# An FFN behind a recurrent cross-attention: the third and fourth weight transfers cut in quarters, batch 0's softmax by quarters, a rewritten opening order

## The chip, the cores and the metric

The kernel runs on one core of a Trainium2 chip. The metric is device time in microseconds (us) of one execution, median over several runs. A profile of one execution goes with it: its "span" is the part in which the core's engines have instructions, and the execution's own time is a little longer. The engines are TensorE (PE in the profile, PEld for its weight loads), VectorE (DVE), ScalarE (ACT), GpSimd (POOL) and SyncE (SP), which only issues transfers. Each runs its own list of instructions in order and waits for others by semaphores.

## What is computed

There are 8 batches of 8 heads, with 512 rows of x and 32 rows of state per head, 64 wide. Two attentions read across: the state rows as queries' partners for x, and the x rows for the state. Their outputs, 544 rows a batch with 8 × 64 = 512 columns, go through a gated FFN of width 1536.

```
scores = scale * x @ state^T            a  = softmax(scores)          xread = a  @ state
scores2 = scale * state @ x^T           a2 = softmax(scores2)         sread = a2 @ x
y = concat([xread, sread], rows)        # 8 * 544 rows of 512 columns
gate = 1 / (1 + exp(-(y @ w_gate)));    val = y @ w_val
out = (gate * val) @ w_out
```

The inputs and the output are float32; the kernel multiplies in bfloat16 and adds up in float32.

## The kernel before

**Work per batch.** Since xread is a @ state, the kernel never forms it: it multiplies state by the gate and value weights first (the tile SW, 256 rows by 2 × 1536), and then SW by a. In steps, by the helpers' names:

- xT: x of a batch, transposed. For batches 0 and 1 by TensorE (`xT_mm`, L132) and a copy out of PSUM (`xT_cp`, L135), for later ones by DMA transposes on SP's queue (`at_xT_dma`, L140), after a cast to bfloat16 (`cast_xp` L91 for batch 0, `cast_x` L116).
- S: scores by TensorE (`S_mm`, L147 and L156), half a batch's heads or rows at a time; `S_exp` (L167, ScalarE) makes the exponentials E1; `n_sum` (L181, L183) sums them and takes the reciprocal on VectorE; `n_mul` (L200) multiplies into ab. `n_sums` and `n_muls` (L187 to L193) do both halves at once.
- aT: ab transposed, by TensorE (`aT_mm` L207, `aT_cp` L217) for batches 0 and 1, by DMA transposes (`aT_dma`, L221) later.
- rd: sread, by `at_Eb` (L173, four casts of E1 on GpSimd), `rd_mm` (L235 to L241) and `rd_fin` (L246, L248).
- SW: `sw_visit(b, lo, n)` multiplies state by n columns of the weights from column lo. Called with w = 0 (gate) or 1 (value) it takes up to 512 columns of one (`sw_mm`, L259); without, 256 columns of both (`sw_pair`, L266). A visit is eight matmuls into two PSUM banks; `sw_cp` (L303) evicts each of the two on ScalarE (act) or VectorE (vec). For batches from 2 on, `sw_wide` makes three visits.
- gv: `gv_mm(b, f, ...)` is the product of SW and aT for 128 of the 1536 columns: two matmuls for the gate, two for the value. `gv_th` (L327) takes tanh on ScalarE, `gv_glu` (L332) joins gate and value on VectorE.
- out: `out_mm` (L348), four matmuls of a third of a 128-row block; after the third, the result is scaled (L352) and stored (L356).

**Transfers.** x of batch 0 and of batches from 4 on come on SP's queue, the first state rows on ScalarE's; everything else on GpSimd's queue: x of batch 1 (`load_xh`, L96), weights with a cast to bfloat16 (`load_w(w, lo, n)`, L100), w_out in three blocks (`load_wo`, L107), state (`load_sb`, L394), x of batches 2 and 3 (`load_x`, L78). These issues stand in GpSimd's list among its casts and multiplications. A transfer of the queue may also wait for the eighth one ahead of it, whose semaphore it takes over.

**Order.** All engines' work is written out by hand: the order of the calls is the order of each engine's list. Ahead of the loop over batches 2 to 8 (from L681) stands one long list of calls (L430 to L680), for all of batches 0 and 1, the outputs of batch 0 and the preparation of batch 2. `warm(n, place)` (L384) puts in n matmuls on zeros. PSUM's eight banks are places: GV (2 banks), OU (1), SWP (4) and AT (1); a matmul into a bank waits for the last reader of what was there. `gate(tile)` (L104) copies one element on GpSimd, so that what stands behind it in GpSimd's list waits for that tile.

The list before opens so: x of batch 0 in quarters of its heads (6, 0, 4, 2), the casts on ScalarE, VectorE and GpSimd, scores in halves of which each is made in two parts, and exponentials, sums and multiplications by halves:

```
    S_mm(0, 1, GV, (0,))
    S_mm(0, 0, SWP, (0,))
    S_mm(0, 1, SWP, (1,))
    S_exp(0, 1)
    n_sum(0, 1)
    S_mm(0, 0, AT, (1,))
```

The weights come as columns 256 to 511 of value and of gate, then 512 columns from 1024 of gate and of value, from 512 of value, from 512 of gate, and the first 256 of each.

Of the kernel before, what the change touches and what calls it, by code (L numbers as in the profile page):

```python
# [16 lines left out]
def kernel(  # L17
# [92 lines left out]
    def zero(t, eng):  # L110
        (nc.gpsimd if eng is pool else nc.vector).memset(t, 0.0)
# [22 lines left out]
    def xT_cp(b, j, cp, n=1):  # L134
        cp(xT_tile(b)[:, j:j + n], held["xT", b, j])  # L135
# [28 lines left out]
    def S_exp(b, i):  # L164
        if b not in E1s:
            E1s[b] = ap_.tile((128, 4, 2, 128), FP, name="E1")
        nc.scalar.activation(half(b, i, E1s), held["S", b, i].rearrange("p c e j n -> p (c e j) n" if b > 1 else "p c e j n -> p (c e) j n"),  # L167
                             AF.Exp, scale=scale)
# [133 lines left out]
    def sw_cp(b, lo, w, e, cp):  # L302
        cp(*sw_left.pop((b, lo, w, e)))  # L303
# [76 lines left out]
    def warm(n, place):  # L380

        ps = place[0].tile((128, 512), FP, name="warm", tag=place[1])
        for _ in range(n):
            nc.tensor.matmul(ps.rearrange("p (r k) -> p r k", r=4), wm, wm.unsqueeze(1).to_broadcast((128, 4, 128)), start=True, stop=True)  # L384
# [12 lines left out]
    def cast_s(q, cp):  # L397
        sbs[q] = stg.tile((128, 1, 4, D), BF, name="sb", bufs=1)
        cp(sbs[q], sfs[q])
# [27 lines left out]

    ident_e = ident.rearrange("p (g e u) -> p e g u", e=2, u=8)
    pre = wp.tile((128, 2), FP, name="pre")
    load_xp(0, nc.sync, 6, 2)  # L430
    nc.vector.memset(wm, 0.0)  # L431
    warm(1, GV)
    warm(2, GV)
    warm(4, SWP)
    zero(sTz, pool)
    load_xp(0, nc.sync, 0, 2)
    load_s(0, nc.scalar)
    zero(sTd, vec)
# [12 lines left out]
    load_w(1, 256, 256)
    cast_xp(0, pool, 4, 2)
    xT_mm(0, 0, GV)
    xT_cp(0, 0, act)
    xT_mm(0, 2, SWP)
    warm(1, SWP)
    xT_cp(0, 3, vec)
    load_w(0, 256, 256)
    xT_cp(0, 2, vec)
    S_mm(0, 1, GV, (0,))  # L460
    load_xp(0, nc.sync, 2, 2)
    S_mm(0, 0, SWP, (0,))
    cast_xp(0, act, 2, 2)
    xT_mm(0, 1, OU)
    zero(sbz, vec)
    xT_cp(0, 1, vec)
    S_mm(0, 1, SWP, (1,))
    warm(1, GV)
    S_exp(0, 1)
    n_sum(0, 1)  # L470
    S_mm(0, 0, AT, (1,))
    warm(1, OU)
    load_w(0, 1024, 512)
    xT_mm(1, 0, SWP, 2)
    warm(2, AT)
    S_exp(0, 0)
    warm(1, SWP)
    warm(1, SWP)
    xT_mm(1, 2, OU, 2)
    xT_cp(1, 0, act, 2)  # L480
    S_mm(1, 0, SWP)
    xT_cp(1, 2, act, 2)
    S_exp(1, 0)
    n_sum(0, 0)
    n_mul(0, 0, vec)
    load_w(1, 1024, 512)
    nc.vector.memset(ones, 1.0)
    at_Eb(0)
    rd_mm(0, GV)
    n_mul(0, 1, vec)  # L490
    S_mm(1, 1, GV)
    S_exp(1, 1)
    aT_mm(0, AT)
    sw_visit(0, 256, 256)
    load_sb(2)
    sw_cp(0, 256, 2, 0, act)
    rd_fin(0)
    aT_cp(0, 0, vec)
    aT_cp(0, 1, vec)
    sw_visit(1, 256, 256)  # L500
    load_w(1, 512, 512)
    sw_cp(0, 256, 2, 1, vec)
    sw_cp(1, 256, 2, 0, act)
    warm(2, OU)
    at_Eb(1)
    n_sums(1)
    gv_mm(0, 2, GV)
    gv_th(0, 2)
    sw_cp(1, 256, 2, 1, act)
    rd_mm(1, OU)  # L510
# [24 lines left out]
    gv_mm(0, 8, SWP)
    gv_glu(0, 11)
    gv_mm(0, 10, GV)
    gv_th(0, 8)
    gv_th(0, 10)
    sw_cp(1, 1024, 1, 1, vec)  # L540
    load_w(1, 0, 256)
    gv_glu(0, 8)
    sT_mm(2, AT)
    sw_visit(1, 512, 512, 1)
    sw_cp(1, 512, 1, 1, act)
    gv_mm(1, 9, SWP)
    gv_th(1, 9)
    sT_cp(2, act)
    gv_mm(1, 11, SWP)
    gv_glu(0, 10)  # L550
    gv_th(1, 11)
    load_x(2, nc.gpsimd)
    rd_fin(1)
    gv_glu(1, 9)
    gv_mm(1, 2, GV)
    sw_cp(1, 512, 1, 0, act)
    sw_visit(1, 512, 512, 0)
    gv_glu(1, 11)
    gv_th(1, 2)
    sw_visit(0, 512, 512, 0)  # L560
    sw_cp(1, 512, 0, 1, act)
    gv_glu(1, 2)
    sT_mm(1, AT)
    sw_cp(1, 512, 0, 0, act)
    sw_cp(0, 512, 0, 1, vec)
    gv_mm(1, 10, GV)
    sw_visit(0, 512, 512, 1)
    gv_th(1, 10)
    sw_cp(0, 512, 0, 0, vec)
    gv_mm(1, 6, SWP)  # L570
    load_wo(1)
    sw_cp(0, 512, 1, 1, act)
    gv_th(1, 6)
    gv_glu(1, 10)
    gv_mm(1, 8, GV)
    sw_cp(0, 512, 1, 0, vec)
    load_wo(0)
    gv_glu(1, 6)
    gv_th(1, 8)
    gv_glu(1, 8)  # L580
    sT_mm(3, OU)
    sw_visit(1, 0, 256)
    sw_cp(1, 0, 2, 0, act)
    sw_visit(0, 0, 256)
    load_wo(2)
    gv_mm(0, 4, GV)
    sw_cp(1, 0, 2, 1, vec)
    sw_cp(0, 0, 2, 0, vec)
    cast_x(2, vec, 0, 4)
    gv_mm(1, 4, SWP)  # L590
    gv_th(0, 4)
    sw_cp(0, 0, 2, 1, act)
    gv_mm(0, 0, SWP)
    gv_glu(0, 4)
    sT_cp(3, act)
    gv_th(0, 0)
    gv_glu(0, 0)
    gv_mm(0, 5, GV)
    gv_mm(1, 7, SWP)
    gv_th(0, 5)  # L600
    gv_glu(0, 5)
    gv_th(1, 7)
    gv_glu(1, 7)
    gv_th(1, 4)
    gv_mm(0, 7, GV)
    gv_th(0, 7)
    gv_glu(0, 7)
    gv_mm(0, 1, SWP)
    gv_th(0, 1)
    gv_mm(1, 1, SWP)  # L610
    gv_glu(0, 1)
    gv_mm(1, 3, GV)
    gv_th(1, 1)
    gv_mm(1, 5, SWP)
    gv_glu(1, 4)
    gv_th(1, 3)
    gv_glu(1, 3)
    sT_cp(1, act)
    gv_mm(0, 6, GV)
    gv_th(0, 6)  # L620
    out_mm(0, 0, AT)
    cast_x(2, pool, 4, 4)
    gv_th(1, 5)
    at_xT_dma(2)
    gv_glu(0, 6)
    out_mm(0, 2)
    out_mm(0, 1, GV)
    gv_mm(0, 9, SWP)
    gv_th(0, 9)
    out_mm(0, 3)  # L630
    gv_glu(1, 5)
    pad(2, 6)
    S_mm(2, 0, GV)
    gv_glu(1, 1)
    gv_glu(0, 9)
    S_exp(2, 0)
    S_mm(2, 1, OU)
    S_exp(2, 1)
    n_sum(2, 0)
    n_sum(2, 1)  # L640
    out_mm(0, 4)
    out_mm(0, 5)
    n_mul(2, 0, vec)
    out_mm(0, 6, GV)
    load_x(3, nc.gpsimd)
    at_Eb(2)
    n_mul(2, 1, pool)
    sw_wide(2, 1)
    sw_cp(2, 1, 1, 0, act)
    aT_dma(2, 0)  # L650
    sw_cp(2, 1, 0, 0, vec)
    rd_mm(2, GV)
    sw_cp(2, 1, 1, 1, act)
    rd_fin(2)
    out_mm(0, 8)
    sw_cp(2, 1, 2, 1, vec)
    gv_mm(1, 0, SWP)
    nc.scalar.activation(pre[:, 0:1], ones, AF.Exp)
    aT_dma(2, 1)
    gv_th(1, 0)  # L660
    sw_cp(2, 1, 2, 0, vec)
    gv_glu(1, 0)
    sw_cp(2, 1, 0, 1, act)
    cast_x(3, pool, 4, 4)
    cast_x(3, act, 0, 4)
    out_mm(0, 7, GV)
    sw_wide(2, 0)
    at_xT_dma(3)
    sw_cp(2, 0, 2, 0, vec)
    out_mm(0, 10)  # L670
    out_mm(0, 9)
    sw_cp(2, 0, 1, 0, act)
    sw_cp(2, 0, 2, 1, act)
    sw_cp(2, 0, 0, 1, vec)
    out_mm(0, 11)
    load_x(4, nc.sync)
    sw_cp(2, 0, 0, 0, vec)
    gate(xTs[2][:, 0, 3, 0:1])
    nc.gpsimd.memset(xs[:, :, :, D:], 1.0)
    sw_cp(2, 0, 1, 1, vec)  # L680

    for b in range(2, B + 1):
        nb = b + 1 if b + 1 < B else None
# [87 lines left out]
```

## Time and profile before

| what | us |
|---|---|
| median of 3 runs | 222.56 (222.18 to 223.69) |
| the profiled execution | 222.21 |
| its span | 220.4 |
| TensorE busy | 214.4 |
| ScalarE busy | 129.0 |
| VectorE busy | 118.1 |
| GpSimd busy | 53.5 |

TensorE's granted clock is at its full value in all 40 slices of the span. In the profile a line such as "L259 PE MATMUL swp<-wgv,sTd 64*32 64x512 bf16" names the line of the kernel, the engine, the operation, the tile written and the tiles read, and the shape. Several records of one kind that follow each other are merged ("x8"). In the chain of waits each piece is the one that released the next, traced back from the last instruction; the tile names in it are those that the piece writes. Matmuls overlap in the pipeline, so one of 512 columns has 0.38 us from start to end while four of them take 0.86 us of the chain.

### The profile page before, as it was taken

What the parts mean: (1) busy time and instruction counts of PE and PEld (TensorE: products, weight loads), DVE (VectorE), ACT (ScalarE), POOL (GpSimd) and SP (SyncE); (2) the same over time, 40 slices, a digit from 0 to 9 for tenths busy, and PEclk for the clock granted to TensorE, in tenths of its full rate; (3) what the DMA queues carried; (4) which work ended last, traced back from release to release, by engine and by line L of the source; (5) the groups of instructions that cost most, each with busy time, mean ns of one, the idle gap of its engine ahead of it and who ended that gap; (6) DMA issues with size and microseconds to landing.
All of it is one profiled execution on the core that took longest, in us unless ns stands there. A gap on an engine that the chain in (4) does not pass through costs nothing.

```text
span 220.4 us, 4641 instructions
## 1 busy us (share of the span) xinstructions
PE 214.4 (97%) x1779; PEld 104.3 (47%) x1801; DVE 118.1 (54%) x209; ACT 129.0 (59%) x241; POOL 53.5 (24%) x90
## 2 busy tenths in 40 slices
PE   8899999999999999999999999999999999999994
PEld 3554444443444444444544454445444444566744
DVE  1899897486366446544574458344844344322301
ACT  4688977367675667565765667476656444432311
POOL 8787010370324054003600090005100000000001
PEclk9999999999999999999999999999999999999999
DMA  6999999853699445947452215230131111111113
GB/s 197 201 204 196 275 221 158 172 176 60 156 272 245 62 117 164 205 120 211 133 157 45 95 23 152 54 113 3 50 93 57 49 54 65 65 57 48 49 34 112
DMA packets 41910, 27.11 MB, mean 123 GB/s; under 512 B 24000, under 2 KB 38080, under 8 KB 41888
## 3 DMA queue, kind: packets, MB, share of 16 engines
q1 hardware_dynamic: 32544, 18.95, 34.4%
q0 software_dynamic: 9056, 7.67, 19.9%
q10 hardware_dynamic: 288, 0.20, 0.6%
q8 instruction: 14, 0.23, 0.5%
q14 instruction: 8, 0.07, 0.2%
HBM read 18.35 MB, written 8.91 MB: 124 GB/s over the span
## 4 chain that ended last, share of the span: by engine, by line
PE 93%; DVE 4%; issue 1%; ACT 1%
PE outp L348 38%; PE gvp L317 38%; PE gvp L320 5%; PE swp L259 4%; PE warm L384 2%; PE swp L266 1%; PE Sp L147 1%; PE outp L370 1%; PE rdp L235 1%; DVE rs L181 1%; DVE ab L193 1%; DVE rs L187 1%; PE aTp L207 1%; PE Sp L156 0%; DVE ab L200 0%
## 5 line engine op out<-in xcount | busy, mean ns | idle before, releaser
L332 DVE SCALAR_TENSOR_TENSOR glu<-th,gvp 128x512 bf16<-128x512 f32 (+1 forms) x108 | 70.4, 656 | 84.4 <-ACT th L327 69.4
L348 PE MATMUL outp<-wo,glu 128*128 128x512 bf16 x374 | 95.7, 379 | 1.2
L317 PE MATMUL gvp<-aT,SW 128*128 128x512 bf16 x384 | 96.7, 380 | 0.0
L327 ACT ACTIVATE th<-gvp 128x512 f32<-128x512 f32 (+1 forms) x108 | 61.7, 575 | 59.7 <-PE gvp L317 47.4
L317 PEld LDWEIGHTS <-SW 128*128 128x128 bf16 x384 | 36.1, 98 | 47.9 <-issue 5.6
L348 PEld LDWEIGHTS <-glu 128*128 128x128 bf16 x396 | 37.9, 98 | 42.1 <-issue 0.4
L303 ACT CAST SW<-swp 128x512 bf16<-128x512 f32 x70 | 39.2, 584 | 6.1 <-PE swp L259 4.7
L352 ACT ACTIVATE res<-outp 128x512 f32<-128x512 f32 x33 | 19.7, 597 | 15.2 <-PE outp L348 15.0
L303 DVE CAST SW<-swp 128x512 bf16<-128x512 f32 x26 | 17.3, 683 | 1.0 <-PE swp L266 0.8
L104 POOL COPY pre<-th 128x1 f32<-128x1 f32 x5 | 0.9, 187 | 69.4 <-ACT th L327 69.4
L361 POOL DMA_DIRECT2D out_dram<-res x2 | 1.1, 549 | 60.4 <-ACT res L352 60.4
L173 POOL CAST Eb<-E 128x256 bf16<-128x256 f32 x32 | 11.7, 400 | 12.9 <-ACT E L167 12.9
L116 POOL CAST xb<-xf 128x1024 bf16<-128x1024 f32 x10 | 10.4, 1059 | 11.1 <-DMA xf<-in_x_dram 7.6
L320 PE MATMUL gvp<-XS,wgv 128*128 128x256 bf16 x96 | 11.9, 273 | 0.0
L320 PEld LDWEIGHTS <-wgv 128*128 128x128 bf16 x96 | 9.4, 98 | 3.0
L167 ACT ACTIVATE E<-Sp 128x512 f32<-128x512 f32 x16 | 9.6, 604 | 1.9 <-PE Sp L147 1.0
L224 POOL CAST xs<-xf 128x1024 bf16<-128x1024 f32 x10 | 10.2, 1045 | 0.0
L181 DVE TENSOR_REDUCE rs<-E 128x16 f32<-128x512 f32 x14 | 9.4, 672 | 1.2 <-ACT E L167 1.2
L200 DVE TENSOR_TENSOR ab<-E,ri 128x512 bf16<-128x512 f32 x13 | 8.9, 696 | 0.0
L259 PE MATMUL swp<-wgv,sTc 64*32 64x512 bf16 x192 | 7.6, 381 | 0.0
L384 PE MATMUL warm<-wm 128*128 128x512 bf16 x17 | 6.4, 497 | 1.0 <-DVE wm L431 1.0
L147 PEld LDWEIGHTS <-xT 128*128 128x128 bf16 x96 | 4.3, 98 | 2.6
(71 smaller groups left out, 93.3 us busy)
## 6 DMA issues: line engine op xcount, KB each, us to landing
out_dram<-res SPq DMA_DIRECT2D x24, 256.0 KB, 3.2
xf<-in_x_dram SPq DMA_DIRECT2D x4, 1024.0 KB, 7.2
xf<-in_x_dram POOLq DMA_DIRECT2D x2, 1024.0 KB, 9.1
out_dram<-res SPq DMA_DIRECT2D x15, 128.0 KB, 1.9
wo<-in_moe_w_out_dram POOLq DMA_DIRECT2D x3, 512.0 KB, 13.9
xf<-in_x_dram SPq DMA_DIRECT2D x4, 256.0 KB, 3.9
wgv<-in_moe_w_gate_dram POOLq DMA_DIRECT2D x2, 512.0 KB, 8.0
wgv<-in_moe_w_val_dram POOLq DMA_DIRECT2D x2, 512.0 KB, 9.5
```

What stands on the lines that cost most here:

```text
L116: cp(xbs[b].rearrange("p c h d -> p h c d")[:, lo:lo + n], (xhs if b in xhs else xfs)[b][:, lo:lo + n])
L173: nc.gpsimd.tensor_copy(Ebs[b][:, c], E1s[b][:, c])
L181: nc.vector.tensor_reduce(grp(b, rs), half(b, i, E1s), AX.X, ALU.add)
L259: nc.tensor.matmul(pss[e][j * Ns:(j + 1) * Ns, o:o + n], sTc[rows, b, j] if b > 1 else sTd[rows, b, 2 * j + e, e], (wg, wv)[w][rows, j, lo ...
L303: cp(*sw_left.pop((b, lo, w, e)))
L317: nc.tensor.matmul(ps, SWs[b][:, g, w, fs], aTs[b][:, :, g], start=(g == 0), stop=(g == 1))
L320: nc.tensor.matmul(ps, (wg, wv)[w][:, j, fs], XS[:, :, j], start=(j == 0), stop=(j == 3))
L327: nc.scalar.activation(th, held["gv", b, f][0], AF.Tanh, scale=0.5)
L332: nc.vector.scalar_tensor_tensor(glus[b][:, f], held["th", b, f], 1.0, held["gv", b, f][1], ALU.add, ALU.mult)
L348: nc.tensor.matmul(ops[b, c], glus[b][:, f, c * 128:(c + 1) * 128], wo[:, f], start=(f == 0), stop=(f == NF - 1))
L352: nc.scalar.activation(res, ops[b, c], AF.Copy, scale=0.5)
L384: nc.tensor.matmul(ps.rearrange("p (r k) -> p r k", r=4), wm, wm.unsqueeze(1).to_broadcast((128, 4, 128)), start=True, stop=True)
```

## The change

Four helpers are new: scores, exponential, sum with reciprocal, and multiplication for a quarter of batch 0's heads (two heads of eight, all rows).

```diff
+    def Sq_mm(b, j, place):
+        ps = held["Sq", b, j] = place[0].tile((128, 4, 2, Ns), FP, name="Sp", tag=place[1])
+        for c in range(4):
+            e, c2 = c // 2, c % 2 * 2
+            nc.tensor.matmul(ps[:, c2:c2 + 2, e], xTs[b][:, j, c], sTd[:, b, 2 * j + e], start=True, stop=True)
+
+    def quarter(b, j, t):
+        return t[b].rearrange("p c e (j n) -> p (c e) j n", n=Ns)[:, :, j]
+
+    def Sq_exp(b, j):
+        if b not in E1s:
+            E1s[b] = ap_.tile((128, 4, 2, 128), FP, name="E1")
+        nc.scalar.activation(quarter(b, j, E1s), held["Sq", b, j].rearrange("p c e n -> p (c e) n"), AF.Exp, scale=scale)
+
+    def nq_sum(b, j):
+        rs = ap_.tile((128, 8), FP, name="rsq", bufs=4)
+        nc.vector.tensor_reduce(rs, quarter(b, j, E1s), AX.X, ALU.add)
+        ri = held["riq", b, j] = ap_.tile((128, 8), FP, name="riq", bufs=4)
+        nc.vector.reciprocal(ri, rs)
+
+    def nq_mul(b, j, eng):
+        if b not in abs_:
+            abs_[b] = ap_.tile((128, 4, 2, 128), BF, name="ab")
+        (nc.gpsimd if eng is pool else nc.vector).tensor_tensor(quarter(b, j, abs_), quarter(b, j, E1s),
+                          held["riq", b, j].unsqueeze(2).to_broadcast((128, 8, Ns)), ALU.mult)
```

The list ahead of the loop is written anew. It has the same products, visits, outputs and warm-up matmuls; what differs is the order, the places, some engines, and the split of four transfers. The loop is untouched. The opening, up to the first products:

```diff
-    load_w(0, 1024, 512)
-    load_w(1, 1024, 512)
...
+    load_xp(0, nc.sync, 6, 2)
+    nc.gpsimd.memset(xs[:, :, :, D:], 1.0)
+    zero(sTd, pool)
...
+    zero(sbz, vec)
+    load_xp(0, nc.sync, 4, 2)
+    cast_xp(0, act, 6, 2)
+    zero(sTz, vec)
...
+    load_xh(1, 0, 4)
+    load_xh(1, 4, 4)
+    load_w(1, 256, 256)
+    load_xp(0, nc.sync, 0, 2)
+    Sq_mm(0, 3, SWP)
+    load_w(0, 256, 256)
+    Sq_exp(0, 3)
+    cast_xp(0, act, 0, 2)
...
+    load_w(1, 1024, 256)
+    Sq_mm(0, 1, SWP)
+    warm(1, GV)
+    nq_sum(0, 3)
+    nq_mul(0, 3, vec)
+    load_w(0, 1024, 256)
+    xT_cp(0, 0, vec)
+    Sq_exp(0, 2)
+    load_sb(2)
...
+    nq_sum(0, 1)
+    load_w(1, 0, 256)
+    nq_sum(0, 0)
+    load_w(0, 0, 256)
+    nq_mul(0, 1, vec)
+    nq_mul(0, 0, vec)
+    nq_mul(0, 2, pool)
+    S_exp(1, 0)
+    xT_cp(1, 2, vec, 2)
+    aT_mm(0, GV)
+    at_Eb(0)
+    n_sum(1, 0)
+    aT_cp(0, 1, act)
+    S_mm(1, 1, GV)
+    S_exp(1, 1)
+    aT_cp(0, 0, vec)
+    warm(1, SWP)
+    sw_visit(0, 256, 256)
+    sw_visit(1, 256, 256)
+    sw_cp(0, 256, 2, 0, act)
+    load_w(0, 1280, 256)
+    rd_mm(0, AT)
+    sw_cp(0, 256, 2, 1, act)
+    n_sum(1, 1)
+    gv_mm(0, 2, SWP)
+    n_mul(1, 0, pool)
+    gv_th(0, 2)
+    n_mul(1, 1, pool)
...
+    gv_mm(0, 3, GV)
+    sw_visit(0, 1024, 256)
+    gv_glu(0, 2)
+    load_w(1, 1280, 256)
+    sw_visit(1, 1024, 256)
```

So the third and fourth weight transfers, 512 columns each from column 1024 (gate, then value), become four of 256 columns: value and gate from 1024, and later gate and value from 1280. The first 256 columns of both now come before the latter two. Batch 1's multiplications go from one on VectorE (`n_muls`) to two on GpSimd (`n_mul`).

Later in the list, the parts that bring up batches 2 and 3:

```diff
-    cast_x(2, vec, 0, 4)
-    cast_x(2, pool, 4, 4)
-    load_x(3, nc.gpsimd)
...
+    load_wo(0)
...
+    load_x(2, nc.gpsimd)
...
+    load_wo(1)
...
+    load_wo(2)
...
+    cast_x(2, pool, 4, 4)
...
+    cast_x(2, pool, 0, 4)
...
+    at_xT_dma(2)
...
+    gate(xTs[2][:, 0, 3, 0:1])
...
+    load_x(3, nc.gpsimd)
...
+    n_mul(2, 0, pool)
...
+    aT_dma(2, 0)
+    n_mul(2, 1, pool)
...
+    aT_dma(2, 1)
...
+    cast_x(3, vec, 4, 4)
+    cast_x(3, act, 0, 4)
...
+    at_xT_dma(3)
```

The `gate` on batch 2's last DMA transpose stands in front of the load of batch 3's x in GpSimd's list; before it stood at the end of the list, behind that load. One cast of batch 2's x goes from VectorE to GpSimd and one of batch 3's from GpSimd to VectorE, and the first multiplication of batch 2 from VectorE to GpSimd. `rd_mm(2)` is at the end of the list now.

More of the change, by code (lines that the diff above doesn't have):

```diff
@@ L554 @@
+    sT_mm(3, AT)
+    gv_th(1, 9)
     gv_glu(1, 9)
[L555 removed]
+    nc.scalar.activation(pre[:, 0:1], ones, AF.Exp)
+    gv_th(0, 4)
+    gv_mm(0, 6, GV)
     sw_cp(1, 512, 1, 0, act)
     sw_visit(1, 512, 512, 0)
[L558 to L569 removed]
@@ L668 @@
[L668 to L680, printed above, removed]
+    sT_cp(3, act)
+    gv_glu(0, 4)
+    sw_cp(1, 512, 1, 1, vec)
+    cast_x(2, pool, 0, 4)
+    gv_th(0, 6)
+    gv_glu(0, 6)
+    gv_mm(0, 5, SWP)
+    at_xT_dma(2)
@@ new lines @@
+    gv_th(1, 6)
+    out_mm(0, 9)
+    sw_cp(1, 1280, 2, 0, act)
+    sw_cp(1, 1280, 2, 1, vec)
+    gv_mm(1, 10, SWP)
+    gv_th(1, 10)
+    out_mm(0, 2)
+    sw_cp(1, 0, 2, 1, vec)
+    sw_cp(1, 0, 2, 0, vec)
+    gv_mm(1, 1, SWP)
+    gv_th(1, 1)
+    load_x(3, nc.gpsimd)
+    gv_glu(1, 10)
+    gv_glu(1, 6)
+    out_mm(0, 4)
+    out_mm(0, 11)
+    S_mm(2, 0, SWP)
+    gv_mm(1, 4, GV)
+    gv_mm(1, 5, SWP)
+    gv_glu(1, 1)
+    S_exp(2, 0)
+    n_sum(2, 0)
+    gv_th(1, 4)
+    gv_th(1, 5)
```

329 lines of the change are left out of this document (136 added, 193 removed).

## The prediction

> **What bounds the kernel now.** I read the page first (span, engine shares, the chain of work that ended last), then the chain in order of time, then TensorE's timeline and the groups of the first 60 us by shape, and last the transfers.
>
> ```profile
> span 220.4 us, 4641 instructions
> PE 214.4 (97%) x1779; PEld 104.3 (47%) x1801; DVE 118.1 (54%) x209; ACT 129.0 (59%) x241; POOL 53.5 (24%) x90
> PE 93%; DVE 4%; issue 1%; ACT 1%
> ```
>
> TensorE is the bound: 93% of the chain. The other engines hold the chain only for some 5% of 220.4 us. Where they do is seen in the chain in order of time (start, duration, what):
>
> ```profile
> 0.99 3.59 PE warm L384 x8
> ...
> 5.80 0.69 DVE sTd L418
> ...
> 7.43 0.41 PE Sp L156 x8
> ...
> 8.21 0.60 ACT E L167
> ...
> 12.90 0.76 DVE aT L217 x2
> 13.66 0.60 DVE SW L303
> ...
> 17.49 0.62 PE aTp L207 x8
> 18.11 0.59 PE swp L259 x16
> ...
> 25.40 0.34 PE stp L410 x8
> 25.74 0.86 PE gvp L317 x4
> 26.60 0.34 PE swp L259 x8
> ```
>
> Until 17.49 us the chain hops between VectorE, ScalarE and TensorE (the softmax of batches 0 and 1); from 17.49 on it is TensorE back to back. The diff touches only the written order ahead of the batch loop. It has as many matmuls as before (17 warm-up ones in both), since two visits of 512 columns with one weight and two visits of 256 columns with gate beside value are the same columns and the same four evictions. So it can win only idle TensorE time ahead of about 27 us, and lose by opening a new hole later. The question is when TensorE has the same work behind it.
>
> **The head, up to the first gate/value product.** TensorE's timeline (start, duration, operation) gives the point of comparison, gv_mm(0, 2), the first product:
>
> ```profile
> 13.91 1.22 PE L317 MATMUL gvp<-aT,SW 128*128 128x512 bf16 x4
> 15.06 0.42 PE L238 MATMUL rdp<-xf,Eb 128*32 128x64 bf16 x32
> 15.41 0.35 PE L241 MATMUL rdp<-ones,Eb 128*128 128x1 bf16 x8
> ```
>
> The groups of the first 60 us, by shape (count, busy us, mean ns of one, idle before):
>
> ```profile
> L303 ACT CAST SW<-swp 128x512 bf16<-128x512 f32 x23 | 12.7, 587 | 2.9 <-PE swp L259 2.1 <-PE swp L266 0.7
> ...
> L181 DVE TENSOR_REDUCE rs<-E 128x16 f32<-128x512 f32 x4 | 2.6, 656 | 1.2 <-ACT E L167 1.2
> ...
> L200 DVE TENSOR_TENSOR ab<-E,ri 128x512 bf16<-128x512 f32 x3 | 2.1, 734 | 0.0
> ...
> L200 POOL TENSOR_TENSOR ab<-E,ri 128x512 bf16<-128x512 f32 x1 | 1.3, 1292 | 0.4 <-DVE ri L183 0.4
> ...
> L193 DVE TENSOR_TENSOR ab<-E,ri 128x1024 bf16<-128x1024 f32 x1 | 1.2, 1210 | 0.0
> L187 DVE TENSOR_REDUCE rs<-E 128x32 f32<-128x1024 f32 x1 | 1.2, 1207 | 0.0
> L135 DVE COPY xT<-xTp 128x512 bf16<-128x512 bf16 x3 | 1.2, 403 | 0.0
> ...
> L183 DVE RECIPROCAL ri<-rs 128x16 f32<-128x16 f32 x4 | 1.0, 253 | 0.1
> ...
> L399 ACT CAST sb<-sf 128x256 bf16<-128x256 f32 x1 | 0.4, 404 | 1.2 <-DMA sf<-in_state_dram 1.2
> ```
>
> The start does not move: the same eight warm-up matmuls run to 4.58, then the state transposes, then the two pads, the second ending at 5.80 + 0.69 = 6.49. The zero fills change engines (sTd to GpSimd, sTz and sbz to VectorE), in front of work that waits for the transfers of x anyway; I cost them at nothing. Batch 0's x is asked for in another order of quarters on the same queue, which changes which quarter comes when, not when the four land. The first scores need only one transposed quarter of x and the pads, so they run at about 6.5 instead of 7.43: 0.9 us won. A quarter's exponential I put at 0.40 (the 256-wide ScalarE row), ready at 7.2, and that is early: VectorE still has a cast of x (as the copy row doubled at most, 0.6) and one xT copy (0.40) behind its pad, to 7.5.
>
> From 7.5 VectorE is the chain. Per quarter, by the slope between the 512 and the 1024 rows: a sum is 0.656 − (1.207 − 0.656)/2 = 0.38, a multiplication 0.734 − (1.210 − 0.734)/2 = 0.50, a reciprocal at most 0.25. Ahead of aT_mm(0) it runs four sums (1.52), four reciprocals (1.01), three multiplications (1.50) and the last xT copy (0.40): 4.4 us, so 11.9. The fourth multiplication, on GpSimd, is half of 1.29 and beside it. Before, aT_mm(0) ran behind rd_mm and S_mm(1, 1) and its copies began at 12.90; here they can begin at about 12.4. Cutting in quarters buys an early start with more instructions, each with its fixed part; half of the 0.9 us is left.
>
> It is then given back. The second pair of batch 1's xT goes from ScalarE to VectorE, behind those multiplications: twice 0.40 as the upper bound, to about 12.6. Then come S_mm(1, 1) (0.41, as the 7.43 row), S_exp(1, 1) (0.60), and, behind it on ScalarE, both evictions of the first weight visit, at 0.587: 12.6 + 0.41 + 0.60 + 1.17 = 14.8, or 14.5 with each neighbour on ScalarE starting 0.1 ahead of the other's end. Before, one eviction was on VectorE (the 13.66 row) and the product started at 13.91. So gv_mm(0, 2) starts 0.6 us **later**. Bounds: 14.1, if each VectorE piece costs 0.1 less, and 15.1, with no overlap anywhere. I take the middle.
>
> **From there to 26.6.** What TensorE has done before between 13.91 and 26.60 is nine products, seven visits of eight matmuls, rd_mm(1), aT_mm(1), and sT_mm twice. Back to back these cost 9 × 0.86 + 7 × 0.30 (half the 18.11 row) + (0.42 + 0.35 − 0.12 of overlap) + 0.62 + 2 × 0.34 = 11.8 us, and took 12.69: 0.9 us was idle, the largest part ahead of aT_mm(1) at 17.49, which waited for VectorE. In the new order aT_mm(1) waits for GpSimd's two multiplications (the second behind a sum and a reciprocal on S_exp(1, 1), which ends at about 13.7: 13.7 + 0.40 for an aT copy + 0.66 + 0.25 + 1.29 = 16.3), while TensorE reaches it at 14.5 + 2 × 0.86 + 2 × 0.30 = 16.8: covered by 0.5 us. The other items in that stretch wait for evictions with 0 to 0.6 us in hand; one, gv_mm(0, 11), is short by about 0.1. I take 0.2 us for new stalls, 0 to 0.8 as bounds. Sum: +0.6 − 0.9 + 0.2 = **−0.1**; with the bounds −0.7 to +1.1.
>
> **Transfers.** Two more weight issues occupy GpSimd (0.75 each, by the first row below), but the queue's length in bytes is the same.
>
> ```profile
> 6.40 1.50 POOL L100 DMA_DIRECT2D wgv<-in_moe_w_gate_dram  x2
> 18.37 0.90 POOL L78 DMA_DIRECT2D xf<-in_x_dram  x1 [0.18 <-issue]
> 19.26 0.77 POOL L107 DMA_DIRECT2D wo<-in_moe_w_out_dram  x1
> 30.09 1.04 POOL L116 CAST xb<-xf 128x1024 bf16<-128x1024 f32 x1 [7.57 <-DMA xf<-in_x_dram]
> ```
>
> ```profile
> wgv<-in_moe_w_gate_dram POOLq DMA_DIRECT2D x1, 256.0 KB, 5.7
> xf<-in_x_dram POOLq DMA_DIRECT2D x1, 1024.0 KB, 11.7
> wo<-in_moe_w_out_dram POOLq DMA_DIRECT2D x1, 512.0 KB, 13.2
> ```
>
> The first gate piece lands at 6.40 + 5.7 = 12.1, ahead of the first visit in both orders. The quarter-sized third and fourth pieces follow at about 1.3 us each, so at 13.4 and 14.7, with products on them only from 16; the weights gain slack. Batch 2's x is now issued behind the first block of wo: it landed at 18.37 + 11.7 = 30.1, and the wo block behind it at 32.5, so 32.5 is where it goes. Both casts are on GpSimd now, 2 × 1.04, so the DMA transposes of batch 2 start at 34.6.
>
> ```profile
> 31.77 5.63 SPq L140 DMA_TRANSPOSE xT<-xb  x4
> ```
>
> ```profile
> xT<-xb SPq DMA_TRANSPOSE x1, 7.4
> xT<-xb SPq DMA_TRANSPOSE x1, 5.2
> ```
>
> ```profile
> 43.45 0.63 PE L147 MATMUL Sp<-sTz,xT 128*128 128x64 bf16 x16
> 54.86 1.04 PE L317 MATMUL gvp<-aT,SW 128*128 128x512 bf16 x4
> ```
>
> Before they started at 31.77 and the last, issued at about 36.2, landed at 41.4, 2 us ahead of the scores at 43.45. Moved by 2.9 us as they are, the first two land by 42.7 and the last by 44.3. The new order calls for the first two at about 42.5 and the last two at 44.3. I cost this at 0.1, since the wo traffic beside which the 7.4 arose ends earlier relative to them. The held x of batch 3 is issued behind that landing (42 to 44 instead of 39.75), lands some 7 us later, and its casts stand on VectorE and ScalarE in front of work wanted from 50 on: VectorE would be blocked with gv_glu(1, 11) queued behind it, but only past about 51. Behind the gate on GpSimd stand this load, n_mul(2, 0), n_mul(2, 1) and the Eb copies, and aT's transposes wait for those; but their inputs come from scores that wait for the same landing, so the gate opens first. No cost. The loop is unchanged.
>
> **The number.** The profiled execution took 222.21 (1.8 around its span), 0.35 under the median of the runs, 222.56. The sum is −0.1 for it, so the median goes to about **222.4**: no change that can be told (a measurement here tells about 1%, 2.2 us).
>
> **Rivals.** *Batch 2 comes late* (slower). If the transposes keep their 7.4 us latency and slip by another 2 to 3 us, the chain scores, exponential, sum, GpSimd multiplication (1.29, on VectorE 0.73 before), two DMA transposes ends behind the point where the loop's first product wants aT (54.86). Counted back from there: about 8 us, so the last xT must land by 46.5; each us beyond costs one. For: the margin shrinks from over 4 to about 2 us, and DVE waits in order behind x of batch 3 too. Against: the 7.4 falls to 5.2 within the one group. Landing at 49 gives 222.4 + 2.5 = 224.9. Chance 0.14.
>
> *The port* (a little slower). The last two VectorE multiplications of batch 0 now run beside GpSimd's four Eb casts. If the two engines exclude each other, each multiplication waits for up to a whole cast, 1.43/4 = 0.36, and aT_mm(0) and all behind it come 0.7 later: 223.1.
>
> ```profile
> 10.68 1.51 DVE L200 TENSOR_TENSOR ab<-E,ri 128x512 bf16<-128x512 f32 x2
> 9.60 1.43 POOL L173 CAST Eb<-E 128x256 bf16<-128x256 f32 x4 [0.96 <-ACT E L167]
> ```
>
> Against it: before, the first of them overlapped the last cast by 0.35 and the pair still took 1.51, near twice 0.73. Chance 0.12. [...]
>
> *The lower bounds hold* (faster, but within 1%). With a product at 14.1 and no stall, 0.6 less; at the earliest it starts at 13.3 (the visit right behind the landing at 12.1, two evictions side by side), 1.4 less. The middle is 221.4. For: every hop is a row. Against: ScalarE has both evictions. Chance 0.14. Nothing in the first 27 us holds 2.2 us to be won, so faster by over 1% needs something that no row shows: 0.05 in all.
>
> **How the numbers follow.** Forecast 0.57, the port 0.12, the lower bounds 0.14, batch 2 late 0.14, and 0.03 for what no row shows. Faster by over 1% takes a little of the lower bounds and of that rest, slower the late batch 2 and a little more. The range reaches from the lower bounds to a landing half as late as in the slow rival: 221.0 to 224.2.
>
> **What would show it.** Right: first scores near 6.5, first product at 14.1 to 15.1 in TensorE's timeline, no hole over 0.3 us between there and 27, and TensorE at the loop's first product (54.86 before) within 1 us. Wrong: TensorE waiting for DMA transposes between 42 and 56, VectorE waiting for x of batch 3, or aT_mm(1) waiting for GpSimd.

## The result, and the profile after

| | median us | runs | ratio to before, 95% interval |
|---|---|---|---|
| before | 222.94 (222.13 to 223.96) | 20 | |
| after | 221.82 (221.64 to 222.99) | 20 | 0.9954 (0.9941 to 0.9967) |
| after, twice more (below) | 222.07 and 222.14 | 12 and 12 | 0.9977 (0.9957 to 0.9996) and 0.9950 (0.9919 to 0.9982) |
| before, against itself (below) | 223.10 | 12 | 1.0026 (1.0004 to 1.0049) |

The change wins 0.5 to 1.1 us, inside the 1% that counts as no change. The last row is a warning: two sets of runs of the same kernel lay 0.26% apart, so a difference of 0.3% between two kernels tells little. Three later runs of after, of 225.22, 226.19 and 225.75 us, were in a slower state with a lower granted clock (0.992, 0.983 and 0.984) and are left out of the ratios; without them the two later medians are 221.91 and 222.02.

The page of after (span, busy time of each engine, shares of the chain that ended last):

```profile
span 220.6 us, 4665 instructions
...
PE 213.8 (97%) x1778; PEld 104.0 (47%) x1801; DVE 118.4 (54%) x213; ACT 130.2 (59%) x245; POOL 57.9 (26%) x95
...
PE 92%; DMA 2%; DVE 2%; ACT 1%; issue 1%; SPq 1%
```

This execution took 222.38 us, *longer* than before's profiled 222.21, although the median fell by 1.1. It lies 0.56 above its median and before's lay 0.73 below its own. So one pair of profiles cannot show the gain; that was the first thing to settle. The chain of waits of after, in order of time (start, duration, what):

```profile
2.26 5.14 DMA xf<-in_x_dram
7.42 0.63 ACT xf L91
8.10 0.41 PE xTp L132 x4
...
10.75 1.05 DVE ab L193 x2
...
11.94 0.62 PE aTp L233 x8
...
13.66 0.98 ACT SW L329 x2
14.69 1.68 PE gvp L343 x7
```

New at its head is a transfer: the last quarter of batch 0's x, asked for at 2.26, lands at 7.40; in before it was asked for at 2.26 too and landed at 6.6. After's timeline (start, duration, engine, operation; in brackets the idle time before and what ended it):

```profile
2.23 1.70 POOL L96 DMA_DIRECT2D xf<-in_x_dram  x2
6.36 0.28 PE L174 MATMUL Sp<-sTd,xT 128*128 128x64 bf16 x4
7.42 0.62 ACT L91 CAST xf<-xf 128x512 bf16<-128x512 f32 x1 [0.37 <-DMA xf<-in_x_dram]
8.10 0.40 PE L132 MATMUL xTp<-ident,xf 128*128 128x128 bf16 x4 [0.67 <-ACT xf L91]
14.20 2.17 PE L343 MATMUL gvp<-aT,SW 128*128 128x512 bf16 x8
41.63 0.19 POOL L104 CAST pre<-xT 128x1 f32<-128x1 bf16 x1 [4.96 <-DMA xT<-xb]
42.43 0.40 PE L147 MATMUL Sp<-sTz,xT 128*128 128x64 bf16 x8
54.77 1.04 PE L343 MATMUL gvp<-aT,SW 128*128 128x512 bf16 x4
65.96 2.48 POOL L116 CAST xb<-xf 128x1024 bf16<-128x1024 f32 x2 [1.83 <-PE gvp L343]
66.67 2.31 DVE L226 TENSOR_TENSOR ab<-E,ri 128x512 bf16<-128x512 f32 x2
69.45 1.18 PE L343 MATMUL gvp<-aT,SW 128*128 128x512 bf16 x4
```

Before's timeline has these rows for GpSimd's first transfer, for VectorE's two multiplications and for GpSimd's two casts:

```profile
2.99 1.70 POOL L96 DMA_DIRECT2D xf<-in_x_dram  x2
66.76 1.29 DVE L200 TENSOR_TENSOR ab<-E,ri 128x512 bf16<-128x512 f32 x2
67.70 2.23 POOL L116 CAST xb<-xf 128x1024 bf16<-128x1024 f32 x2 [3.50 <-PE gvp L317]
```

The first scores come at 6.36, the first product at 14.20 (13.91 before), the loop's first product at 54.77 (54.86 before). The last three rows of after's timeline are a surprise in a loop that the diff does not touch: VectorE's two multiplications take 2.31 us (1.29 before, at 66.76) beside GpSimd's two casts, and the product at 69.45 takes 1.18 where its neighbours take 1.03.

### The profile page after: what moved, and what is told of

It reads as the page before. It is cut to its first block, busy times and chain, and to the rows that moved or that the text cites. A ratio compares the mean times of both kernels' runs of the same rounds, so it can differ in the third digit from the quotient of the medians.

```text
span 220.6 us, 4665 instructions
## 1 busy us (share of the span) xinstructions
PE 213.8 (97%) x1778; PEld 104.0 (47%) x1801; DVE 118.4 (54%) x213; ACT 130.2 (59%) x245; POOL 57.9 (26%) x95
## 4 chain that ended last, share of the span: by engine, by line
PE 92%; DMA 2%; DVE 2%; ACT 1%; issue 1%; SPq 1%
PE gvp L343 38%; PE outp L374 38%; PE gvp L346 5%; PE swp L285 3%; DMA xf<-in_x_dram 2%; PE swp L292 2%; PE Sp L147 1%; PE outp L396 1%; PE rdp L261 1%; SPq L83 1%; PE aTp L233 1%; DVE rsq L186 1%; DVE ab L193 0%; ACT SW L329 0%; PE rdp L264 0%
## 5 line engine op out<-in xcount | busy, mean ns | idle before, releaser
L199 POOL CAST Eb<-E 128x256 bf16<-128x256 f32 x32 | 12.2, 419 | 7.1 <-ACT E L167 7.1
L167 ACT ACTIVATE E<-Sp 128x512 f32<-128x512 f32 x14 | 8.5, 604 | 0.7 <-PE Sp L156 0.5
L226 DVE TENSOR_TENSOR ab<-E,ri 128x512 bf16<-128x512 f32 x10 | 7.8, 787 | 0.0
```

The lines of the kernel that those rows point to most:

```text
L199: nc.gpsimd.tensor_copy(Ebs[b][:, c], E1s[b][:, c])
```

## The experiments

All twelve were timed in five rounds against the kernel before, in three groups, each on one chip; before's own median in the groups was 222.63 (e1 to e4), 222.98 (e5 to e8) and 222.84 (e9 to e12). "After" is the changed kernel, and "the gated kernel" is after with one wait more in the loop (e5 and e12). The traced executions are put side by side first, because the argument goes by them (us; "lost in the loop" is how much later the product near 173 us stands, against the loop's first product, than in before's profile):

| execution | first product | loop's first product | lost in the loop | span |
|---|---|---|---|---|
| before, profile | 13.91 | 54.86 | 0 | 220.4 |
| before again (e1) | 14.04 | 54.98 | 0 | 220.6 |
| before + loop gate (e6) | 14.96 | 55.72 | 0 | 221.3 |
| before, half of x read twice (e9) | 14.41 | 55.76 | 0.63 | 222.0 |
| after, profile | 14.20 | 54.77 | 0.26 | 220.6 |
| after again (e2) | 13.83 | 54.40 | 0.79 | 220.8 |
| after again (e11) | 13.74 | 54.32 | 0.62 | 220.5 |
| after + loop gate (e5) | 13.48 | 54.39 | 0.12 | 220.1 |
| after + loop gate (e12) | 13.74 | 54.32 | 0.12 | 220.0 |

**Both kernels again, unchanged.** 

> The kernel before, unchanged, for a second profiled execution and for how far two sets of runs of one kernel lie apart. All theories: ratio 1.000 within 0.15%. Theory 'just in time' (an ordinary execution of before waits for data in the opening that its profiled one, 0.7 us under the median, did not wait for): an execution near the median of 222.9 shows TensorE at the loop's first product at about 55.5 instead of 54.86, and the 0.6 us as idle TensorE time ahead of 27 us, released by a DMA or by a cast of a landed tile. Rival 'batches 2 and 3': the same 0.6 us lies between 27 and 54 us. Rival 'the loop': the first product stays at 54.9 and the 0.6 us lies behind it.

> The changed kernel, unchanged, for a second profiled execution. Its profiled one lay 0.56 us above its median, before's 0.73 below its own, so the two profiles are 1.3 us nearer to each other than the medians. All theories: ratio 0.995 to 0.996. Theory 'just in time': an execution near 221.8 has the loop's first product at about 54.2 instead of 54.77, and its last quarter of x lands ahead of 7.40. Rival 'the loop': the first product stays near 54.8, and the rest of the span is 0.5 us shorter.

Before's second execution took 222.32, the least of its runs, and tells nothing of those near 224. After's second took 222.57, so it is not the execution near 221.8 that the expectation asked for. It has the loop's first product at 54.40, near the 54.2 of the first theory, and then loses more than the 0.46 won, 0.51 of it in one wait at 70 us. So the traced executions of the two kernels are near to each other because after's come ahead and then stumble in the loop.

**x of batch 3 not held.**

```diff
-    gate(xTs[2][:, 0, 3, 0:1])
+    load_x(3, nc.gpsimd)
     gv_glu(0, 7)
...
-    load_x(3, nc.gpsimd)
+    gate(xTs[2][:, 0, 3, 0:1])
     gv_glu(1, 10)
```

> The changed kernel with the load of batch 3's x issued where its gate stood (at about 36.7 us of the profile instead of 42.2) and the gate put where the load stood. Theory 'the hold pays' (x of batch 3 beside the DMA transposes of batch 2 delays these): the last transpose lands at 43 or later instead of 41.6, the scores of batch 2 wait, and the time is 0.5 to 1.5 us above the changed kernel's. My prediction's step (the hold costs nothing) and the rival 'the hold does nothing': within 0.2 us of the changed kernel.

Median 222.27, ratio 0.9980 (0.9963 to 0.9998), against 222.07 and 0.9977 for after in the same group. GpSimd's timeline shows when batch 2's last DMA transpose has landed (the gate's copy):

```profile
44.62 0.19 POOL L104 CAST pre<-xT 128x1 f32<-128x1 bf16 x1 [6.89 <-DMA xT<-xb]
```

The scores that need the last transposes, in TensorE's timeline of the same execution:

```profile
44.30 0.53 PE L147 MATMUL Sp<-sTz,xT 128*128 128x64 bf16 x8
```

The load does delay the transposes, by 3.0 us (41.63 in after), and uses up nearly all the slack: the scores take 0.53 us instead of the 0.40 of after's profile, so TensorE stood some 0.13 there, and from the first product to the loop's first it is 40.71 us (14.11 to 54.82) against 40.57. The hold buys 3 us of slack and, in this execution, 0.1 us of time. The medians differ by 0.2, or by 0.36 without after's two runs above 225; the two intervals overlap.

**The weights' third and fourth transfers joined again.**

```diff
-    load_w(1, 1024, 256)
+    load_w(1, 1024, 512)
-    load_w(0, 1024, 256)
+    load_w(0, 1024, 512)
-    load_w(0, 1280, 256)
-    load_w(1, 1280, 256)
```

> The changed kernel with the third and fourth weight transfers again of 512 columns each (value, then gate, from column 1024), in the places of the first two quarter transfers; the visits and the order stay. Theory 'the quarters serve the order' (the visit at 16.30 needs gate columns that then land at about 18.0 instead of 15.4): 1.0 to 1.8 us slower than the changed kernel, with TensorE idle ahead of that visit. Rival 'the split is of no account' (the gain is from the softmax by quarters and the order of the visits alone): within 0.2 us of the changed kernel.

Median 225.27, ratio 1.0117 (1.0095 to 1.0139): 3.2 us above after, about twice the price expected. TensorE's timeline:

```profile
18.31 1.06 PE L292 MATMUL swp<-wgv,sTd 64*32 64x512 bf16 x16 [2.55 <-DMA wgv<-in_moe_w_gate_dram]
19.30 1.03 PE L233 MATMUL aTp<-ident,ab 128*128 128x128 bf16 x8
20.57 3.33 PE L343 MATMUL gvp<-aT,SW 128*128 128x512 bf16 x12
```

The window of 18 to 22 us of the same execution (busy time of each engine; the third number from the end is TensorE's granted clock):

```profile
18.00:22.00 4.00, 3.69 (x36) 1.98 (x37) 1.89 (x3) 2.44 (x4) 4.00 (x7) 0.57 1.33 201
```

The wait is 2.55 us. Behind it the same 16 matmuls take 1.06 instead of the 0.63 of after's profile, 8 transposes 1.03 instead of 0.62 and 12 matmuls 3.33 instead of 2.75: the granted clock is 0.57 in this window, and those three rows alone cost 1.4 us more. The new order cannot do without the quarter transfers.

**GpSimd's casts of batch 4's x made to wait for VectorE's multiplications,** in after and in before.

```diff
                 if f == (6 if nb == 3 else 1) and nb + 1 < B:
+                    if nb == 3:
+                        gate(abs_[3][:, 3, 1, 127:128])
                     cast_x(nb + 1, pool, 0, 4)
```

> The changed kernel with one line more in the loop: GpSimd's two casts of batch 4's x wait for VectorE's second multiplication of batch 3 (a gate on its last element). Theory 'collision at 66 us' (the changed order lets batch 4's x land 1.5 us earlier, at 65.4 to 66.1 instead of 67.5; GpSimd's casts then start just ahead of VectorE's two multiplications at 66.3 to 66.7, the pair takes 1.9 to 2.8 us instead of 1.3, and TensorE waits 0.1 to 0.7 us at 69 to 70): the pair takes 1.3 us, no hole at 69 to 70, the spread of the runs shrinks, median 0.2 to 0.6 us below the changed kernel's, 221.5. Rival 'the two only happen to stand beside each other': the pair stays above 1.8 us or the hole stays, and the median does not move.

> The kernel before with the same gate. Theory 'collision' (in before batch 4's x lands at about 67.5, while the multiplications run from 66.8 to 68.0, so an earlier landing in one execution or another makes them collide, and this is before's spread of 222.1 to 224): the runs close up to 222.1 to 222.5, median 0.4 to 0.7 us under before's, and the changed kernel's lead goes down to the 0.1 to 0.5 us by which it is ahead at the loop's first product. Rival 'before's spread comes from the opening': spread and median stay, ratio 0.999 to 1.001.

> The changed kernel, unchanged, on the same chip as the gated one. Ratio to before 0.995 to 0.998; if the collision at 66 us matters in ordinary executions, its median is 0.1 to 0.5 us above the gated kernel's, and its trace shows the two multiplications at 1.9 us or more.

> The gated changed kernel again, on the same chip as the changed kernel. Collision theory: 0.1 to 0.5 us under it and with the narrower spread. Rival 'the collision is hidden in ordinary executions': the two medians agree within 0.1 us.

The two executions e11 and e12 are twins up to 66 us (first product 13.74, loop's first 54.32) and differ only in the gate. The timeline of e11 around 66 us (GpSimd, VectorE, TensorE):

```profile
65.86 2.48 POOL L116 CAST xb<-xf 128x1024 bf16<-128x1024 f32 x2 [2.19 <-PE rdp L261]
66.21 2.67 DVE L226 TENSOR_TENSOR ab<-E,ri 128x512 bf16<-128x512 f32 x2
69.94 0.59 PE L343 MATMUL gvp<-aT,SW 128*128 128x512 bf16 x2 [0.34 <-DVE glu L358]
```

The timeline of e12, at the same place and, in the first two lines, in the opening:

```profile
10.10 1.84 POOL L199 CAST Eb<-E 128x256 bf16<-128x256 f32 x4
10.43 0.91 DVE L193 TENSOR_TENSOR ab<-E,riq 128x256 bf16<-128x256 f32 x2
...
66.22 1.29 DVE L226 TENSOR_TENSOR ab<-E,ri 128x512 bf16<-128x512 f32 x2
67.83 2.02 POOL L116 CAST xb<-xf 128x1024 bf16<-128x1024 f32 x2
69.00 1.03 PE L343 MATMUL gvp<-aT,SW 128*128 128x512 bf16 x4
```

Without the gate the pair takes 2.67 us, with it 1.29; the wait at 69.94 is gone, and the span is 0.5 shorter (220.0 against 220.5). The collision and its price are shown for this pair of executions. In the medians it is not: 222.14 for after (222.02 without the run at 225.75), 222.17 gated (0.9950 and 0.9980, intervals that overlap); the earlier gated group had 221.84 (0.9951, 0.9922 to 0.9980). A likely reason stands in the list of runs. After's three traced executions took 222.38, 222.57 and 222.28, but 14 of its first 20 runs took 221.64 to 221.98, near e12's 221.80. So the traced executions seem to be the ones that collide, and most others not to pay for it; none of those near 221.8 was traced without the gate, so this is not shown. Before with the gate: 222.76, ratio 0.9995 (0.9971 to 1.0018), runs from 222.26 to 223.87; the rival was right, before's spread has another source.

One such source stands in e6's timeline:

```profile
11.07 0.62 PE L132 MATMUL xTp<-ident,xf 128*128 128x128 bf16 x8 [0.72 <-DMA xf<-in_x_dram]
13.85 0.63 PE L266 MATMUL swp<-wgv,sTd 64*32 64x512 bf16 x16 [0.20 <-DMA wgv<-in_moe_w_gate_dram]
14.96 1.04 PE L317 MATMUL gvp<-aT,SW 128*128 128x512 bf16 x4
```

The window of 7.5 to 11 us of e6 shows that the transfers themselves were slower (the last number is GB/s moved by all DMA engines):

```profile
7.50:11.00 3.50, 2.62 (x34) 1.47 (x31) 3.11 (x7) 2.21 (x3) 2.39 (x7) 1.00 1.22 156
```

The same window of before:

```profile
7.50:11.00 3.50, 3.27 (x50) 2.36 (x50) 3.11 (x7) 2.29 (x4) 2.54 (x7) 1.00 1.44 194
```

In e6 the DMA engines moved 156 GB/s in that stretch instead of 194, the second half of batch 1's x came 0.7 us too late, and the loop began 0.86 us later than in before's profile: the whole difference of the two spans.

**Before without that wait.**

```diff
-                h, c = 2 * (j + jj) + k // 2, k % 2 * 2
+                h, c = (2 * (j + jj) + k // 2) % (4 if b == 1 else 8), k % 2 * 2
```

> The kernel before, in which batch 1's second pair of transposes reads the first half of batch 1's x again (so the scores of batch 1's heads 4 to 7 are made from x of heads 0 to 3); every instruction and transfer stays, only the wait for the second half's landing is gone from TensorE at 10.3. Theory 'just in time' (before's ordinary execution waits there, 0.7 us in the one traced at 223.07, because GpSimd's queue brings the second half anywhere from 9.1 to 11.0): the runs close up toward 222.2, median 0.4 to 0.7 us under before's, ratio 0.997 to 0.998. Rival 'before's spread is elsewhere (batch 0's x, weights, batch 4's x)': median within 0.2 us of before's and the spread stays.

Median 222.81, ratio 0.9993 (0.9960 to 1.0027), runs from 222.19 to 224.59: nothing won. The timeline of its traced execution (223.74 us) says why:

```profile
13.30 0.62 PE L266 MATMUL swp<-wgv,sTd 64*32 64x512 bf16 x16 [0.31 <-DMA wgv<-in_moe_w_gate_dram]
16.59 0.41 PE L259 MATMUL swp<-wgv,sTd 64*32 64x512 bf16 x8 [0.51 <-DMA wgv<-in_moe_w_gate_dram]
67.42 2.48 POOL L116 CAST xb<-xf 128x1024 bf16<-128x1024 f32 x2 [2.33 <-PE rdp L235]
67.65 2.80 DVE L200 TENSOR_TENSOR ab<-E,ri 128x512 bf16<-128x512 f32 x2
71.50 0.59 PE L317 MATMUL gvp<-aT,SW 128*128 128x512 bf16 x2 [0.47 <-DVE glu L332]
```

The next two pieces of the same queue were late instead: the first weights (0.31) and the 512 gate columns (0.51). And before collides at 67 us too, when batch 4's x happens to land early. My theory that one landing makes before's spread has fallen; what e6 and e9 share is a queue whose pieces are wanted one after another with little to spare.

The granted clock, averaged over a run, tells more of before's slowest runs. In the three groups 13 of its 99 runs have a mean of 0.992 or less; they took 223.52 to 224.80, and no other run took over 224.16. In e4, e7 and e8 a mean of 0.992 belongs to the traced execution, with one stretch of some 3 us at half clock (0.50) behind a long wait of TensorE. That the slowest runs of before had such a wait is likely; none of them was traced.

**The last quarter of batch 0's x on ScalarE's queue; batch 0's sums and multiplications by halves.** Both on the gated kernel.

```diff
     load_s(0, nc.scalar)
+    load_xp(0, nc.scalar, 0, 2)
...
-    load_xp(0, nc.sync, 0, 2)
```

```diff
-    nq_sum(0, 3)
-    nq_mul(0, 3, vec)
...
-    nq_sum(0, 2)
+    n_sum(0, 1)
+    n_mul(0, 1, vec)
...
-    nq_sum(0, 1)
...
-    nq_sum(0, 0)
+    n_sum(0, 0)
...
-    nq_mul(0, 1, vec)
-    nq_mul(0, 0, vec)
-    nq_mul(0, 2, pool)
+    n_mul(0, 0, vec)
```

> The gated changed kernel, with the last quarter of batch 0's x (heads 0 and 1) asked for on ScalarE's queue behind the first state rows instead of as the fourth on SP's queue. Theory 'the last quarter bounds the opening' (it lands at 7.0 to 7.4, because its issue at 2.26 is behind GpSimd's first transfer of batch 1's x): it lands by 6.3, TensorE's waits ahead of 8.1 shrink, and the first product comes 0.3 to 0.7 us earlier, at 13.2 to 13.6; the first visit then meets its weights at 12.7, so no more than that is won. Rival 'the DMA engines are full there': the last quarter lands no earlier, or the others land as much later, and the first product stays at 13.8 to 14.2.

> The gated changed kernel, with the sums and multiplications of batch 0 by halves (scores and exponentials stay by quarters; all multiplications on VectorE). My prediction's step (four sums, four reciprocals, three multiplications cost 4.0 us on VectorE, their fixed parts giving back half of the gain): halves cost 2 x (0.66 + 0.25 + 0.73) = 3.3 us, so the first product comes no later, or up to 0.3 us earlier. Rival 'quarters pay because each starts as its exponential is there': the second half waits for the last exponential at 10.05 and needs 1.6 us behind it, so batch 0's transposed a comes 0.2 to 0.6 us later, and so does the first product.

On ScalarE's queue: median 222.23, ratio 0.9975 (0.9949 to 1.0000), 0.4 above the gated kernel of the group. In the traced execution, one of four from 223.04 up, the second and third quarters land at about 5.7 and 6.5 (4.9 and 5.6 in e12), TensorE waits 1.21 us for the second, and the first product comes at 15.15: the rival, at a higher price than it had. Seven of the twelve runs took 222.20 to 222.23, and none of those was traced. By halves: 223.25, ratio 1.0015 (0.9982 to 1.0049), in two groups of runs (222.23 to 222.66, and 223.17 to 224.85; the five from 224.25 up have a mean clock of 0.991 to 0.992). The timeline of e8:

```profile
7.91 0.66 DVE L91 CAST xf<-xf 128x512 bf16<-128x512 f32 x1 [1.36 <-DMA xf<-in_x_dram]
8.63 0.60 PE L132 MATMUL xTp<-ident,xf 128*128 128x128 bf16 x4 [1.75 <-DVE xf L91]
9.42 0.62 ACT L91 CAST xf<-xf 128x512 bf16<-128x512 f32 x1 [2.12 <-DMA xf<-in_x_dram]
```

Its window behind the wait, with the clock third from the end:

```profile
9.00:12.00 3.00, 2.78 (x19) 1.43 (x17) 1.23 (x3) 1.77 (x4) 0.74 (x1) 0.50 1.45 196
```

TensorE's longest wait in e7:

```profile
6.45 0.40 PE L132 MATMUL xTp<-ident,xf 128*128 128x128 bf16 x4 [1.21 <-DVE xf L91]
```

And the window behind it:

```profile
7.50:10.50 3.00, 3.00 (x23) 1.84 (x23) 2.54 (x10) 1.96 (x5) 1.89 (x4) 0.50 1.43 193
```

In e8's execution the third and fourth quarters of x landed at about 7.9 and 9.4, TensorE waited 1.75 us and then ran at a granted clock of 0.50, and the first product came at 16.83. That is the landing, not the halves, so e8 tells little of these. What can be read: from the end of the last exponential to the end of the last multiplication it is 1.74 us by halves (12.76 to 14.50) and 1.52 by quarters (9.82 to 11.34 in e12), and the fastest run is 0.47 slower than the gated kernel's fastest. Both speak for the quarters, weakly.

**The zero fills exchanged.**

```diff
-    zero(sTd, pool)
+    zero(sTz, pool)
...
-    zero(sTz, vec)
+    zero(sTd, vec)
```

> The gated changed kernel with the two zero fills of GpSimd and VectorE exchanged (the 1.8 us fill is again on GpSimd, as in the kernel before), so GpSimd issues batch 1's x at about 3.1 instead of 2.23. Theory 'the zero fills were not free' (their move brings GpSimd's first transfer forward by 0.76 us, beside the end of batch 0's x, whose last quarter lands at 6.9 to 8.9 instead of 6.5): the last quarter lands by 6.6, TensorE's waits for casts of x ahead of 8.1 fall under 0.3 us together, the first product comes at 13.1 to 13.6, median 0.1 to 0.5 us under the gated kernel's. Rival 'all bytes must pass anyway': batch 1's x and the first weights land 0.5 to 0.8 later in exchange, the first visit waits for them, and the median stays or is up to 0.5 us above.

Median 222.79, ratio 0.9986 (0.9956 to 1.0015), 0.6 above the gated kernel of the group. The last quarter of x landed at 6.6, as expected. But that brought TensorE nothing: ScalarE's cast of it began only at 7.39, behind an exponential, and not for want of x (7.20 in e12), and TensorE still waited 0.42 for it, at 8.05, where under 0.3 was expected. The loss is in the timeline further on (ScalarE, VectorE, GpSimd, TensorE):

```profile
7.39 0.61 ACT L91 CAST xf<-xf 128x512 bf16<-128x512 f32 x1
...
10.62 1.94 DVE L193 TENSOR_TENSOR ab<-E,riq 128x256 bf16<-128x256 f32 x2
10.63 1.65 POOL L199 CAST Eb<-E 128x256 bf16<-128x256 f32 x4
...
12.71 0.61 PE L233 MATMUL aTp<-ident,ab 128*128 128x128 bf16 x8 [1.15 <-DVE ab L193]
```

Batch 0's last two multiplications and GpSimd's Eb casts start within 0.01 us of each other, and the pair takes 1.94 where it takes 0.91 in e12, in which the casts began 0.33 earlier. TensorE waits 1.15. So in this execution the exchange brings a collision and no gain from the earlier x; four of the twelve runs took 221.98 to 222.34 and may have escaped it. Nothing that beats the changed kernel came out of these runs.

## Why the prediction was right, and which steps were not

**The bound and the count: right.** TensorE is 92% of the chain, and nothing else became the bound.

**"The start does not move", with the order of x's quarters and the zero fills costed at nothing: wrong.** The scores did come at 6.36 (6.5 forecast). But the shorter fill on GpSimd brings its first transfer from 2.99 to 2.23, beside the tail of batch 0's x, and the last quarter lands at 7.40 in the profile and at about 6.9 in e5, e11 and e12, instead of 6.6. TensorE's wait of 0.67 at 8.10 is on the chain. This is the step that failed: I looked at the queue's length in bytes and not at what a transfer started 0.76 us earlier is beside. Its price is small and not in every execution. ScalarE's cast of that quarter waited 0.37 for it in after's profile and 0.30 in e3; in e2, e4, e5, e11 and e12 it did not wait for it, and in e10, where the fill was moved back, the quarter landed at 6.6 again and nothing was won by it.

**VectorE's chain of 4.4 us from 7.5: right in start, too long.** In e12 it runs from the first sum at 7.39 to the end of the last multiplication at 11.34, 3.95 us. A sum took 0.41 (0.38 forecast), a reciprocal 0.20 (at most 0.25), the last two multiplications 0.45 each (0.50), the copy 0.42 (0.40), and neighbours overlap a little (the sum at 9.30 starts 0.08 before the reciprocal of 9.18 ends).

**The first product at 14.5 (14.1 to 15.1): too late.** 14.20 in the profile, 13.48 to 13.83 in e2, e5, e11 and e12, and 14.11 in e3, which waited for x as the profile did. VectorE's chain ended 0.6 early (above). Batch 1's xT copy took 0.68, not 0.80, and began at 11.26 in e12; and the two evictions that I stacked behind S_exp(1, 1) take 0.98 in the chain, not 1.17.

**"0.9 us was idle" between the first product and 26.6: mis-sized.** From first product to the loop's first it is 40.95 us before and 40.57 after (also in e2, e11 and e12, to 0.01): 0.38 won, where −0.9 + 0.2 said 0.7. In e5, with the earliest first product, it is 40.91, because a wait of 0.27 for gate weights at 24.76 takes back what came early. Before's window from 13.91 to 26.60, for TensorE alone (length, busy time, clock, DMA share, GB/s):

```profile
13.91:26.60 12.69, 12.60 (x165) 1.00 1.39 219
```

TensorE is busy 12.60 of these 12.69 us; nor did it wait ahead of aT_mm(1), since the row before it ends at 17.42 and it starts at 17.49. So the idle time that the step counted on was not there in this form: the 11.8 us of dense work was too little. Three products in a row take 2.70 to 2.87 us of before's chain where I counted 3 × 0.86 = 2.58. Where the 0.38 comes from is not separated. The two errors, product 0.3 too late and idle time 0.3 too large, cancel, and the forecast −0.1 is what the profiles show (54.86 to 54.77). That agreement is luck, and luck of the traced execution too: in e2, e5, e11 and e12 the same product comes 0.5 earlier than before's.

**The transfers: right.** x of batch 2 landed at 33.0 (32.5 forecast), the last transpose at 41.6 (44.3 at the latest), and the scores at 42.43 did not wait; the hold cost nothing. VectorE did stand 2.7 us idle for x of batch 3, up to 51.05, with nothing of TensorE's behind it; I had named that wait as a sign of being wrong, and it cost nothing. The rival *batch 2 comes late* is out.

**"The loop is unchanged", and the rival *the port*: half wrong.** The rival was priced in the opening at 0.7, and a pair of rows was held against it (1.51 for two multiplications, near twice 0.73). That the two engines share a port is shown by no run; the runs show in its place how long the multiplications took beside the casts: 1.94 us instead of 0.91 in e10, where the two start 0.01 apart, and 2.80 instead of 1.29 in e9's loop, 0.23 behind the casts. In after's profile the opening paid 0.2 (1.13 for the pair), and the loop 0.26. What I did not look for was that batch 4's x, asked for at the same time (59.4), lands 1.8 us earlier than before, 65.8 instead of 67.6, and frees GpSimd's casts into VectorE's multiplications; why it lands earlier is not shown. Even with the gate the loop loses 0.12 (e5 and e12); where that comes from was not looked for. In the loops of after's profile, e11 and e9 VectorE begins 0.71, 0.35 and 0.23 us behind the casts and ends 3.02 to 3.03 us after their start, where one after the other the two would take 2.02 + 1.29 = 3.31. Where VectorE starts first, the traces differ: in before's profile it is 0.94 ahead and takes its 1.29, and the casts take 2.23; in e10 it is 0.01 ahead and takes 1.94 all the same.

**From the profile to the median: wrong.** I carried over before's 0.35 us between its profile and its median of three runs. With 20 runs that distance is 0.73, and after's is −0.56. Typical executions of after therefore lie between the forecast and the rival *the lower bounds hold* (221.4). By the table, undisturbed openings bring the loop's first product 0.5 us earlier (54.32 to 54.40 against 54.86 and 54.98), and before loses another 0.9 in two of four traced executions (e6, and e9 with its changed transposes), with waits for late pieces of GpSimd's queue. That this is the whole gain of the medians is argued from nine traces, not shown.

## What to carry to other kernels

A step that changes nothing but where a zero fill runs can move a queue's first transfer (here from 2.99 to 2.23 us); ask what it is then beside, and whether anything waits for what comes late. When an engine off the path starts earlier, look at what it runs next to, up to the first iterations of an untouched loop. And compare several profiles of each kernel before explaining a difference smaller than the spread of the runs, and see from the list of runs which of them a profile stands for.

## What the runs showed of the hardware

- TensorE's granted clock fell to 0.50 behind idle times of 1.21 (e7, 0.50 from 7.5 to 10.5 us), 1.75 (e8, from 9 to 12) and 2.55 us (e4, from 19 to 21), for about 3 us each, and stayed at 1.00 behind 1.15 (e10, from 12.5 to 16) and 0.72 us (e6, from 11 to 14). In these executions the longer waits are thus paid for again, by 1.4 us in e4. In e7 the clock fell only some 0.6 us after the wait had ended (1.00 from 6 to 7 us, 0.55 from 7 to 8); what decides when it falls is not shown.
- VectorE's two multiplications of 128x512 took 1.29 us with none of GpSimd's casts beside them (e12), and 2.31, 2.67 and 2.80 when the two casts of 128x1024 had started 0.71, 0.35 and 0.23 us ahead of them (after's profile, e11, e9); the casts took 2.48 instead of 2.02 in these three. In e2 and e3 the page gives the ten such multiplications a mean of 840 and 743 ns, against 684 in e12, so the ten took 1.56 and 0.59 us longer.
- Between 7.5 and 11 us, with the same transfers of GpSimd's queue in flight, the DMA engines moved 194 GB/s in before's profile and 156 in e6.
